# Two of the first expert's three slots, computed while the last gates still run

## The chip, the cores and the metric

The kernel runs on one core of one Trainium2 chip. The metric is the device time of one execution in microseconds (us). Lower is better. A slot, below, is a group of up to 128 tokens of one expert.

## The reference

Attention (4 batches, 8 heads, 576 tokens, 64 columns, the 32 largest scores of each row kept), then a dense layer, then a layer of eight experts of which each token uses one:

```
x = attn_out.transpose(0, 2, 1, 3).reshape(2304, 512)
h = x @ w_in                                   # 512 -> 2048
y = (h * clip(h + 3, 0, 6) / 6) @ w_out        # 2048 -> 512
logits = y @ w_gate                            # 8 experts
expert = argmax(logits); gate_w = softmax(logits)[expert]
out[t] = gate_w[t] * (relu(y[t] @ w1[expert]) @ w2[expert])   # 512 -> 1024 -> 512
```

## The kernel before

Everything is float32. A product is made of three matmuls on numbers split into a high and a low part (`h`, `l`): high by high, high by low, low by high.

**The dense layer** goes over nine blocks of 256 tokens, each in 16 steps of 128 hidden columns. `moe_step` does one step: 12 matmuls of 256 columns into `l1ps` (`l1`, L851), the activation on ACT, DVE and POOL (`gf`, `gh`, `gl`), and six matmuls of 512 columns into `yps` (`l2`, L882). At a block's end ACT copies its two groups of 128 tokens out (`y`, L889).

**The gate** (`gate`) is run for each group of 128 tokens, a part of it in each `gate_step`: four transposes and ACT copies (L902, L903), logits (L910), arg max and softmax on DVE and ACT, two prefix matmuls that give the token's place within its expert (L934, L935), the row `y` to DRAM (`yd`), and the token's number written to a list in DRAM, `td`, at its place (`to_table`, L960).

**The table.** After the last group, `td` is read back into `trow`, the last block's own places are added by PE out of `placed` (`place`, `in128`, which L953 and L955 make), experts are ranked by size (L1169 to L1175), and `tabg` and `tab` (L1184, L1185) list the tokens of each expert's slots. The largest expert is not first: expert 0 is, at rank 0, and the others follow by rank. `ROOM` gives each rank its columns, 384 for the first two, and a slot is at most 128 of them.

**The experts.** `xgather` fetches the rows of an expert's slots from `yd`, one DMA of POOL for each slot (L1200). `xprep` transposes a slot and splits it (`xeh`, `xel`, L1210 to L1213). `m2l1` makes 12 matmuls into `lp` for each of eight `f` steps (L1229), ACT and DVE make `hh` and `hl` of them (L1233, L1234), and `m2l2`, two steps later, makes three matmuls a slot into `ops` (L1246). `m2out` scales a slot on ACT (`osb`, L1253), and POOL scatters it to the output.

**Expert weights** come in eight pieces an expert, each 512 KB: `wload_` loads one into one of three `raw` tiles through SP's queue (L992, L995), and `wpiece` splits it on ACT (`wh`, L1008) and DVE (`wl`, L1009). Pieces 0, 2, 4, 6 are `w1` and 1, 3, 5, 7 are `w2`; piece 2k or 2k+1 serves steps `f` = 2k and 2k+1. Before, `w1` pieces have five tiles of `wh` and of `wl`, and `w2` pieces six. Expert 0's first six pieces are prepared inside the loop of the last steps, the last two after the table's gather.

What sets the order is a scheduler: it takes instructions by a priority that the code sets (`pr`, `tc.cur_priority`), and each engine then executes its own list strictly in that order, waiting where an operand isn't ready.

Of the kernel before, what the change touches and what calls it, by code (L numbers as in the profile page):

```python
# [39 lines left out]
NRAW = 3  # L40
# [17 lines left out]
def attention_two_moe_kernel(  # L58
# [81 lines left out]
    def r_(ap):  # L140
        return ap.bitcast(F32)
# [78 lines left out]
    def body(cs, exact):  # L220
# [9 lines left out]
        m1p = m1.enter_context(tc.tile_pool(name="m1p" + X, bufs=1))  # L230
        ps1 = m1.enter_context(tc.tile_pool(name="ps1" + X, bufs=1, space=PSUM))
        at = ExitStack()
# [651 lines left out]
        def yevac(bk):  # L884
            pr("yevac")
            ys = []
            for tt in range(TB // P):
                y = m1p.tile([P, YW], F32, tag="ysb", bufs=NRAW, name=f"y{bk}_{tt}")
                A.activation(y[:, 0:DM], yps[tt], AF.Copy, scale=1.0 / 6.0)  # L889
                ys.append(y)  # L890
            return ys

        def gate(bk, tt, y):
            pr("gate")
            i = bk * (TB // P) + tt
            last = bk == NBLK - 1
            yt = (wp[0] if last else m1p).tile([P, NCC, P], F32, tag="yt", bufs=1 + last, name=f"yt{i}")
            for hf in range(2):
# [46 lines left out]
            V.tensor_copy(ad, sc[:, 3:4])  # L945
            if last:

                ad2 = m1p.tile([P, 1], I32, tag="ad2", bufs=2, name=f"ad2{i}")
                place, in128 = [wp[0].tile([P, n], F32, tag=f"oh{n}", bufs=2, name=f"oh{n}_{i}") for n in (P, NSL)]
# [48 lines left out]
        def wpiece(e, i):  # L998
            kind, pc = i % 2, i // 2
            if (e, i) not in wraw:  # L1000
                wload_(e, i)
            raw = wraw.pop((e, i))
            late = kind and pc >= NPC // 2
            nb = 3 if kind else 5
            pool = tabp[0] if late else wp[0]
            h = pool.tile([P, 4 * FW], F32R, tag=f"wh{kind}", bufs=nb, name=f"wh{e}_{i}")
            l = pool.tile([P, 4 * FW], F32R, tag=f"wl{kind}", bufs=nb, name=f"wl{e}_{i}")
# [133 lines left out]
        wp[0] = m2.enter_context(tc.tile_pool(name="wp" + X, bufs=1, side="right"))  # L1141
        pre, order = [], [0, 2, 4, 6, 1, 3, 5, 7]
        while gpos[0] < NG + 3 or pend:
            pr0[0] += STEP
            run(moe_step())
            gate_step()
            tc.cur_priority = pr0[0] + STEP
            if gdone[0] == NTT - TB // P and not trows:
                load_table()
            if gpos[0] > NG - 13 and len(pre) < NPC + NPC // 2:  # L1150

                if len(wraw) == 3 or len(pre) + len(wraw) == NPC + NPC // 2:
# [9 lines left out]
        ps2 = m2.enter_context(tc.tile_pool(name="ps2" + X, bufs=1, space=PSUM))  # L1162
# [18 lines left out]
        V.scalar_tensor_tensor(trows[0], tq, part[:, 3:4], cs["row"][0:NSL, :], op0=ALU.subtract, op1=ALU.subtract)  # L1181
        tps = ps2.tile([P, NSL], F32, tag="tp", bufs=2, name="tps")
# [35 lines left out]
        def m2l1(e, f):  # L1218
# [29 lines left out]
        def m2out(e):  # L1248
            gw = xst[e][2]
            for j in range(slots(e)):  # L1250
                m = slot(e, j)
                o = tabp[0].tile([P, DM], F32, tag="osb", bufs=3, name=f"osb{e}_{j}")[0:m]
                A.activation(o, ops_[j][0:m], AF.Copy, scale=gw[0:m, j:j + 1])  # L1253
                si = G.indirect_dma_start(out, bass.IndirectOffsetOnAxis(tab[0:m, e * SLOTS + j:e * SLOTS + j + 1], 0), o, None,
                                          bounds_check=NT - 1, oob_is_err=False)
                tc.declare_no_dep(si.ins, group="out" + X, reason="no token is in two slots")
                tc.add_to_no_dep_group("out" + X, si.ins)

# [146 lines left out]
```

## Time and profile before

| | |
|---|---|
| median of 3 runs | 1214.06 us (1214.02 to 1214.12) |
| the profiled execution | 1211.3 us, its span 1209.4 us |
| mean granted TensorE clock | 0.959 |
| PE busy | 1118.6 us (92%) |
| DVE, ACT, POOL busy | 934.9, 809.0, 459.0 us |

The span is what the trace covers; the rest of an execution, 1.9 us here, lies around it. Start times below are us from the span's start. Engines: PE is TensorE's matmul, PEld its weight loads, DVE the vector engine, ACT the scalar engine, POOL is GpSimd, and SP issues most DMAs.

### The profile page before, as it was taken

What the parts mean: (1) busy time and instruction counts of PE and PEld (TensorE: products, weight loads), DVE (VectorE), ACT (ScalarE), POOL (GpSimd) and SP (SyncE); (2) the same over time, 40 slices, a digit from 0 to 9 for tenths busy, and PEclk for the clock granted to TensorE, in tenths of its full rate; (3) what the DMA queues carried; (4) which work ended last, traced back from release to release, by engine and by line L of the source; (5) the groups of instructions that cost most, each with busy time, mean ns of one, the idle gap of its engine ahead of it and who ended that gap; (6) DMA issues with size and microseconds to landing.
All of it is one profiled execution on the core that took longest, in us unless ns stands there. A gap on an engine that the chain in (4) does not pass through costs nothing.

```text
span 1209.4 us, 24024 instructions
## 1 busy us (share of the span) xinstructions
PE 1118.6 (92%) x7410; PEld 999.2 (83%) x7410; DVE 934.9 (77%) x3821; ACT 809.0 (67%) x2085; POOL 459.0 (38%) x667
## 2 busy tenths in 40 slices
PE   5677688999999999999999999999998799999995
PEld 4566577788899899999988899999887699888894
DVE  4999999999999999998998899998442544444441
ACT  4787878788778788787777788777442444444441
POOL 5886655743322444422343332322353312112110
PEclk9678899999999999999999999999999799999998
DMA  3664566554544555743444554543583755555430
GB/s 77 198 182 135 171 200 209 143 157 135 152 127 127 134 145 154 169 140 114 124 127 139 117 151 134 129 144 103 172 258 109 217 173 175 155 180 185 145 104 17
DMA packets 184122, 179.23 MB, mean 148 GB/s; under 512 B 123629, under 2 KB 148509, under 8 KB 183984
## 3 DMA queue, kind: packets, MB, share of 16 engines
q1 hardware_dynamic: 178960, 167.24, 48.0%
q0 software_dynamic: 3872, 10.08, 2.5%
q8 instruction: 61, 1.00, 0.4%
q14 instruction: 77, 0.63, 0.2%
q10 hardware_dynamic: 1152, 0.28, 0.1%
HBM read 159.53 MB, written 18.61 MB: 147 GB/s over the span
## 4 chain that ended last, share of the span: by engine, by line
PE 74%; DVE 16%; ACT 5%; issue 2%; DMA 1%; POOL 1%; SPq 0%; ACTq 0%; POOLq 0%; DVEq 0%
PE l1ps L851 14%; PE yps L882 14%; PE ops L1246 10%; PE lp L1229 10%; PE ptps L777 9%; PE sps L618 5%; PE ptps L743 4%; DVE cd L648 2%; DVE pbuf L727 2%; DVE z L684 2%; DVE z L719 2%; PE ptps L910 1%; DVE cw L659 1%; DVE m L654 1%; PE misc L462 1%
## 5 line engine op out<-in xcount | busy, mean ns | idle before, releaser
L882 PE MATMUL yps<-wo,gh 128*128 128x512 f32 x576 | 216.5, 417 | 0.5 <-POOL qh L474 0.4
L286 POOL TENSOR_SCALAR gh<-gf 128x256 fp32r<-128x256 f32 x144 | 73.6, 511 | 343.6 <-PE yps L882 215.3
L648 DVE MAX8 cd<-sbuf 128x8 f32<-128x72 f32 x1152 | 187.9, 218 | 3.0 <-ACT sbuf L288 2.7
L851 PE MATMUL l1ps<-xh,wih 128*128 128x256 f32 x576 | 167.4, 291 | 4.5 <-DVE gf L863 2.4
L851 PE MATMUL l1ps<-xh,wil 128*128 128x256 f32 x576 | 163.8, 284 | 0.0
L851 PE MATMUL l1ps<-xl,wih 128*128 128x256 f32 x576 | 163.6, 284 | 0.0
L777 PE MATMUL ptps<-vn,pt 128*128 128x65 f32 (+1 forms) x1152 | 143.6, 278 | 0.0
L777 PEld LDWEIGHTS ptps<-vn,pt 128*128 128x128 f32 x1152 | 140.9, 198 | 0.0
L1009 DVE TENSOR_TENSOR wl<-raw,wh 128x1024 fp32r<-128x1024 f32 x64 | 78.3, 1231 | 79.6 <-ACT wh L1008 71.1
L727 DVE SCALAR_TENSOR_TENSOR pbuf<-sbuf,tall,pbuf 128x576 f32<-128x576 f32 x144 | 138.8, 964 | 0.1
L871 POOL TENSOR_TENSOR gl<-gf,gh 128x256 fp32r<-128x256 f32 x144 | 125.4, 871 | 11.4
L851 PEld LDWEIGHTS l1ps<-xh,wih 128*128 128x128 f32 x576 | 110.0, 191 | 15.2 <-DVE gf L863 7.2
L882 PEld LDWEIGHTS yps<-wo,gh 128*128 128x128 f32 x576 | 107.2, 189 | 16.7 <-POOL qh L474 0.9
L882 PE MATMUL yps<-wo,gl 128*128 128x512 f32 x288 | 116.8, 406 | 0.6 <-POOL gl L871 0.6
L709 ACT ACTIVATE jk<-sbuf,uall 128x576 bf16<-128x576 f32 x144 | 111.7, 775 | 4.2 <-DVE j L723 0.9
L700 ACT ACTIVATE pbuf<-sbuf,nb 128x576 f32<-128x576 f32 x144 | 111.1, 775 | 4.1 <-PE ptps L745 0.9
L851 PEld LDWEIGHTS l1ps<-xl,wih 128*128 128x128 f32 x576 | 110.1, 191 | 4.1
L288 ACT ACTIVATE sbuf<-sps 128x576 f32<-128x576 f32 x144 | 93.0, 646 | 28.8 <-PE sps L618 18.2
L1008 ACT ACTIVATE wh<-raw 128x1024 fp32r<-128x1024 f32 x64 | 67.3, 1059 | 66.1 <-PE lp L1229 31.7
L743 PE MATMUL ptps<-ident,pbuf 128*128 128x128 f32 x576 | 94.9, 288 | 17.6 <-DVE j L723 12.1
L857 ACT ACTIVATE gf<-l1ps,three 128x256 f32<-128x256 f32 x144 | 67.9, 472 | 64.1 <-PE l1ps L851 51.2
L851 PEld LDWEIGHTS l1ps<-xh,wil 128*128 128x128 f32 x576 | 110.4, 192 | 0.1
(237 smaller groups left out, 3006.1 us busy)
## 6 DMA issues: line engine op xcount, KB each, us to landing
wo<-wod SPq DMA_DIRECT2D x144, 512.0 KB, 3.8
raw<-in_moe_w_dram SPq DMA_DIRECT2D x64, 512.0 KB, 3.7
vn<-in_v_dram SPq DMA_DIRECT2D x96, 128.0 KB, 2.7
rawi<-in_moe_w_in_dram SPq DMA_DIRECT2D x16, 512.0 KB, 4.2
rawo<-in_moe_w_out_dram SPq DMA_DIRECT2D x16, 512.0 KB, 4.2
wod<-wc SPq DMA_DIRECT2D x16, 512.0 KB, 5.7
qn<-in_q_dram SPq DMA_DIRECT2D x126, 64.0 KB, 2.9
yd<-y SPq DMA_DIRECT2D x18, 258.0 KB, 5.0
```

The lines of the kernel that those rows point to most:

```text
L288: A.activation(dst, src, AF.Copy)
L648: V.max(cd[:, c, :], s[:, c * CK:(c + 1) * CK])
L700: A.activation(d["p"], d["s"], AF.Exp, bias=d["nb"], scale=SCALE)
L709: A.activation(jk, d["s"][:, 0:S], AF.Sign, bias=ts[t]["u"], scale=-1.0, accum_out=d["sg"])
L727: V.scalar_tensor_tensor(d["p"], d["s"], tall[:, t:t + 1], d["p"], op0=ALU.is_ge, op1=ALU.mult)
L743: PE.transpose(ptps[:, c * P:(c + 1) * P], pb[:, c0 + c * P:c0 + (c + 1) * P], ident)
L777: PE.matmul(d_, a_, b_, start=(i == 0), stop=(i == len(mm) - 1))
L851: PE.matmul(dst, a[:, c, fs], b_[:, c, :], start=(n == 0), stop=(n == 3 * NCC - 1))
L871: G.tensor_tensor(gl, gf, r_(gh), op=ALU.subtract)
L882: PE.matmul(yps[tt], a[:, tsl], b_, start=(f == 0 and m == 0), stop=(f == NF1 - 1 and m == 2))
L1229: PE.matmul(lp, a[:, c, fs], b_[:, c, 0:w], start=(n == 0), stop=(n == 3 * NCC - 1))
L1246: PE.matmul(ops_[j][0:slot(e, j)], a[:, js], b_[:, ns], start=(f == 0 and m == 0), stop=(f == NF2 - 1 and m == 2))
```

## The change

Expert 0's three slots are split. Slots 0 and 1 are filled from the first eight blocks alone, as soon as those are gated: `early_gather` makes a two-column table by PE (from the list of blocks 0 to 6, read from DRAM at the loop's start, and from `placed` for block 7), gathers 256 rows, and `early_prep` transposes them into the idle half of the dense layer's `xbuf`. `early_l1` and `early_l2` then compute them in the dense layer's PSUM (`l1ps`, `yps`), ahead of the table in the code or beside it by priority. What remains of expert 0 (`room(0)` is 128 columns now) is a second pass through all of its weights. The last table no longer reads what blocks 7 and 8 scattered: PE adds both from `placed`. The gate gets two more steps a loop while blocks remain. `wh` and `wl` have four tiles for each kind of piece, and the next expert's pieces are loaded two steps and split four steps into the second pass.

```diff
+    AHEAD = SLOTS - 1
+    def room(r):
+        return ROOM[r] - (r == 0) * AHEAD * P
...
-            if last:
+            if bk >= NBLK - 2:
...
+        def early_gather():
...
+            ops0 = misc([P, AHEAD])
+            for i, a_ in enumerate(trows):
+                PE.matmul(ops0, a_, ident[0:NSL, 0:AHEAD], start=(i == 0), stop=False)
+            for i, (a_, b_) in enumerate(placed):
+                PE.matmul(ops0, a_, b_[:, 0:AHEAD], start=False, stop=(i == len(placed) - 1))
...
+            for j in range(AHEAD):
+                x = m1p.tile([P, YW], F32, tag="ysb", bufs=NRAW, name=f"xa{j}")
+                G.indirect_dma_start(x, None, yd[0:NT - TB, :], bass.IndirectOffsetOnAxis(fg[:, j:j + 1], 0))
+        def early_prep():
...
+                for c in range(NCC):
+                    PE.transpose(tp[:, c, :], x[:, c * P:(c + 1) * P], ident)
...
+        def early_l1(f):
...
+            for c in range(NCC):
+                for a, b_ in ((h, xh), (h, xl), (l, xh)):
+                    PE.matmul(lp, a[:, c, fs], b_[:, c, :], start=(n == 0), stop=(n == 3 * NCC - 1))
...
+            A.activation(hh, lp, AF.Relu)
+            V.scalar_tensor_tensor(hl, lp, 0.0, r_(hh), op0=ALU.max, op1=ALU.subtract)
+        def early_l2(f):
...
+            for j in range(AHEAD):
+                for m, (a, b_) in enumerate(((hh, h), (hl, h), (hh, l))):
+                    PE.matmul(yps[j], a[:, js], b_[:, ns], start=(f == 0 and m == 0), stop=(f == NF2 - 1 and m == 2))
...
-            late = kind and pc >= NPC // 2
-            nb = 3 if kind else 5
-            pool = tabp[0] if late else wp[0]
-            h = pool.tile([P, 4 * FW], F32R, tag=f"wh{kind}", bufs=nb, name=f"wh{e}_{i}")
+            h = wp[0].tile([P, 4 * FW], F32R, tag=f"wh{kind}", bufs=NPC, name=f"wh{e}_{i}")
...
+        load_table()
         while gpos[0] < NG + 3 or pend:
             run(moe_step())
             gate_step()
+            if gpos[0] < NG:
+                gate_step()
+                gate_step()
-            if gdone[0] == NTT - TB // P and not trows:
-                load_table()
+            if gdone[0] == NTT - TB // P and "x" not in ex_:
+                early_gather()
+            if gpos[0] >= NG - 1 and "gw" not in ex_:
+                early_prep()
...
+        for i in order[len(pre) + len(wraw):]:
+            wload_(0, i, ex_["y"])
...
+        pieces = [(e, i) for e in range(1, NE) for i in range(2 * NPC)]
+        for i in range(2):
+            wload_(*pieces[i])
+        xgather(1)
+        for f in range(NF2 + 1):
+            if f < NF2:
+                early_l1(f)
+            if f:
+                early_l2(f - 1)
+            if f == NF2 - 3:
+                xprep(0, 0)
+        for j in range(AHEAD):
+            send(tabp[0].tile([P, DM], F32, tag="osb", bufs=3, name=f"osa{j}"), yps[j], ex_["gw"][:, j:j + 1], ex_["to"][:, j:j + 1])
+        m1s.close()
+        ps2 = m2.enter_context(tc.tile_pool(name="ps2" + X, bufs=1, space=PSUM))
...
-            if s < len(seq) and e + 1 < NE:
-                wpiece(e + 1, f)
+            if 4 <= s < len(pieces) + 4:
+                wpiece(*pieces[s - 4])
+            if 2 <= s < len(pieces):
+                wload_(*pieces[s])
```

Lines move: in the kernel after the change `l1` is L861, `l2` L892, the table L1250 to L1269, `wh` L1082, `wl` L1083, `xprep` L1293 to L1297, `lp` L1312, `hh` and `hl` L1316 and L1317, `ops` L1329, `osb` L1339, and the early pass L1038 (`l1ps`), L1042 (`ha`), L1043 (`la`) and L1053 (`yps`).

Three places show how instructions move. The first is PE's list at the table, before: the second of the last two gates, the table, and the first gathered slot follow each other.

```order
L934 MATMUL ptps_139<-oh17_14400,tri_86 128x8
L935 LDWEIGHTS ones_94
L935 MATMUL ptps_139<-ohsum_123,ones_94 128x8
L1169 LDWEIGHTS ones_94
L1169 MATMUL rk_14461<-ohsum_123,ones_94 24x8
L1178 MATMUL tq_14468<-trow0_14241,ident_79 24x128
...
L1180 MATMUL tq_14468<-oh128_17_14443,oh24_17_14444 24x128
L1183 MATMUL tps_14474<-place_110,trow0_14241 128x24
L1186 MATMUL rk_14461<-place_110,part_107 1x8
L1210 MATMUL tp0_0_14578<-ident_79,xg0_0_14556 128x128 x4
```

The same place on PE after the change (`la`, `ha` are the early pass's `hl`, `hh`):

```order
L946 MATMUL ptps_142<-ohsum_123,ones_94 128x8
L1053 MATMUL yps_141<-wh0_1_14225,ha0_14648 128x512
L1053 MATMUL yps_141<-wh0_1_14225,la0_14649 128x512
L1053 MATMUL yps_141<-wl0_1_14226,ha0_14648 128x512
L1250 LDWEIGHTS ones_94
L1250 MATMUL ptps_142<-ohsum_123,ones_94 24x8
L1053 MATMUL yps_141<-wh0_1_14225,ha1_14664 128x512
L1259 MATMUL ptps_142<-trow0_13806,ident_79 24x128
...
L1261 MATMUL ptps_142<-place17_14500,in128_17_14501 24x128
L1264 MATMUL ptps_142<-place_110,trow0_13806 128x24
L1038 MATMUL l1ps_140<-xh1_151,wh0_2_14128 128x256
```

The early pass's first two `f` steps stand among the gates, its third `l1ps` behind the table's last large matmul (L1264).

DVE's list at the table, before:

```order
L1172 SCALAR_TENSOR_TENSOR place_110,part_107<-place_110,own_106 24x8
L1173 TENSOR_SCALAR place_110,part_107<-place_110,part_107 24x8
L1174 TENSOR_SCALAR part_107<-part_107 24x1
L1181 SCALAR_TENSOR_TENSOR trow0_14241<-tq_14468,part_107,row_102 24x128
L1175 TENSOR_SCALAR place_110<-row_102,part_107 24x24
```

DVE's list at the table, after:

```order
L1253 SCALAR_TENSOR_TENSOR place_110,part_107<-place_110,own_106 24x8
L1083 TENSOR_TENSOR wl0_5_14616<-raw0_5_14509,wh0_5_14615 128x1024
L1254 TENSOR_SCALAR place_110,part_107<-place_110,part_107 24x8
L1262 SCALAR_TENSOR_TENSOR trow0_13806<-ptps_142,part_107,row_102 24x128
L1255 TENSOR_SCALAR part_107<-part_107 24x1
L1083 TENSOR_TENSOR wl0_7_14620<-raw0_7_14512,wh0_7_14619 128x1024
L1256 TENSOR_SCALAR place_110<-row_102,part_107 24x24
```

Two weight pieces now stand between the rows that make `place`.

ACT's list at expert 0's first steps, before:

```order
L1233 ACTIVATE hh0_0_14615<-lp0_0_14602 128x384
L1008 ACTIVATE wh1_0_14621<-raw1_0_14619 128x1024
L1233 ACTIVATE hh0_1_14647<-lp0_1_14634 128x384
L1008 ACTIVATE wh1_1_14653<-raw1_1_14651 128x1024
L1233 ACTIVATE hh0_2_14670<-lp0_2_14657 128x384
L1008 ACTIVATE wh1_2_14685<-raw1_2_14683 128x1024
L1233 ACTIVATE hh0_3_14702<-lp0_3_14689 128x384
```

ACT's list in the second pass, after (DVE's `hl` and `wl` stand in the same order):

```order
L1082 ACTIVATE wh1_0_14942<-raw1_0_14623 128x1024
L1316 ACTIVATE hh0_1_14866<-lp0_1_14853 128x128
...
L1082 ACTIVATE wh1_4_15062<-raw1_4_14946 128x1024
L1316 ACTIVATE hh0_5_14969<-lp0_5_14956 128x128
...
L1082 ACTIVATE wh1_6_15134<-raw1_6_15014 128x1024
L1316 ACTIVATE hh0_7_15029<-lp0_7_15016 128x128
L1082 ACTIVATE wh1_5_15102<-raw1_5_14980 128x1024
L1316 ACTIVATE hh1_0_15055<-lp1_0_15042 128x384
L1082 ACTIVATE wh2_0_15206<-raw2_0_15066 128x1024
L1316 ACTIVATE hh1_1_15090<-lp1_1_15077 128x384
L1339 ACTIVATE osb0_0_15097<-ops0_14833,gw0_14610 128x512
```

The next expert's `wh` stand ahead of the `hh` of steps 1, 5 and 7, and each of them takes the tile of expert 0's piece of the same kind, so `wh1_0` can be written only when `lp0_1`'s matmuls are done with `wh0_0`.

## Rows read from the trace of the kernel before

**Rows 1.** Chain of waits, 926 to 960 us (start us, length us, what)

```profile
926.99 0.02 issue
...
934.38 0.15 PE ptps L934
...
936.93 5.77 DMA td<-tok,ad
...
949.64 5.58 PE lp L1229 x24
```

**Rows 2.** Windows: stretch, length, PE, PEld, DVE, ACT, POOL busy, clock, DMA, GB/s

```profile
930.00:935.00 5.00, 2.86 (x19) 2.53 (x19) 2.11 (x21) 2.09 (x10) 0.40 (x2) 0.68 0.01 3
...
940.00:950.00 10.00, 4.42 (x18) 3.51 (x18) 1.84 (x3) 2.11 (x4) 6.80 (x13) 0.50 0.81 219
950.00:960.00 10.00, 10.00 (x51) 9.37 (x50) 7.33 (x9) 6.81 (x9) 2.66 (x4) 0.89 0.92 305
```

**Rows 3.** Chain of waits, 976 to 1030 us: expert 1 begins

```profile
980.94 2.08 PE lp L1229 x12
...
991.29 2.05 PE ops L1246 x9
...
997.48 0.44 PE tp L1210 x4
```

**Rows 4.** Chain of waits, 840 to 960 us: the dense layer's last blocks

```profile
859.06 1.96 PE ptps L777 x18
...
896.20 0.79 PE ptps L910 x8
...
917.15 1.38 PE yps L882 x6
918.53 1.43 PE l1ps L851 x12
```

**Rows 5.** Groups by line and shape, 905 to 1210 us (count, busy us, mean ns)

```profile
L1009 DVE TENSOR_TENSOR wl<-raw,wh 128x1024 fp32r<-128x1024 f32 x58 | 70.6, 1225 | 74.7 <-ACT wh L1008 68.2 <-PE ops L1246 3.3 <-PE lp L1229 2.9
L1008 ACT ACTIVATE wh<-raw 128x1024 fp32r<-128x1024 f32 x58 | 61.0, 1059 | 64.8 <-PE lp L1229 31.7 <-DMA raw<-in_moe_w_dram 22.3 <-PE ops L1246 7.2
L1229 PEld LDWEIGHTS lp<-xel,wh 128*128 128x128 f32 x256 | 48.5, 189 | 2.1 <-DVE xel L1213 0.2
L1200 POOL DMA_INDIRECT xg<-yd,tabg x22 | 24.3, 1105 | 65.9 <-PE tp L1210 50.7 <-issue 8.9 <-DVE hl L1234 3.6
L1233 ACT ACTIVATE hh<-lp 128x256 fp32r<-128x256 f32 x16 | 6.1, 381 | 20.8 <-PE lp L1229 20.8
L1234 DVE SCALAR_TENSOR_TENSOR hl<-lp,hh 128x256 fp32r<-128x256 f32 x16 | 6.7, 422 | 20.8 <-ACT hh L1233 20.8
L1246 PEld LDWEIGHTS ops<-wl,hh 128*64 128x64 f32 x24 | 3.2, 135 | 2.4
```

**Rows 6.** Timeline of DVE at the table (start, length, line, operation)

```profile
936.33 0.28 DVE L1172 SCALAR_TENSOR_TENSOR place<-place,own 24x8 f32<-24x8 f32 x1
...
937.35 0.34 DVE L1181 SCALAR_TENSOR_TENSOR trow<-tq,part,row 24x128 f32<-24x128 f32 x1 [0.23 <-issue]
937.62 0.25 DVE L1175 TENSOR_SCALAR place<-row,part 24x24 f32<-24x24 f32 x1
```

**Rows 7.** Timeline of SP's queue and of ACT: two weight loads and what they release

```profile
952.51 0.38 SPq L995 DMA_DIRECT2D raw<-in_moe_w_dram  x1
953.75 0.37 SPq L992 DMA_DIRECT2D raw<-in_moe_w_dram  x1
...
956.38 1.06 ACT L1008 ACTIVATE wh<-raw 128x1024 fp32r<-128x1024 f32 x1 [0.62 <-DMA raw<-in_moe_w_dram]
958.96 1.06 ACT L1008 ACTIVATE wh<-raw 128x1024 fp32r<-128x1024 f32 x1 [0.20 <-DMA raw<-in_moe_w_dram]
```

**Rows 8.** Page, DMA issues (count, size, median us to landing)

```profile
raw<-in_moe_w_dram SPq DMA_DIRECT2D x64, 512.0 KB, 3.7
```

**Rows 9.** Chain of waits at the end: the last expert's slots leave

```profile
1194.09 0.63 ACT osb L1253
...
1194.77 0.70 ACT osb L1253
...
1195.51 0.19 PE ctlp L1296 x2
```

More of the change, by code (lines that the diff above doesn't have):

```diff
@@ L230, in body @@
         m1p = m1.enter_context(tc.tile_pool(name="m1p" + X, bufs=1))
-        ps1 = m1.enter_context(tc.tile_pool(name="ps1" + X, bufs=1, space=PSUM))
+        m1s = ExitStack()
+        ps1 = m1s.enter_context(tc.tile_pool(name="ps1" + X, bufs=1, space=PSUM))
+        m1w = ExitStack()
+        w1p = m1w.enter_context(tc.tile_pool(name="m1w" + X, bufs=1))
         at = ExitStack()
@@ L890, in yevac @@
                 ys.append(y)
+            ex_["y"] = y
             return ys
@@ L896, in gate @@
             last = bk == NBLK - 1
-            yt = (wp[0] if last else m1p).tile([P, NCC, P], F32, tag="yt", bufs=1 + last, name=f"yt{i}")
+            yt = (wp[0] if last and tt else m1p).tile([P, NCC, P], F32, tag="yt", bufs=1, name=f"yt{i}")
             for hf in range(2):
@@ L945, in gate @@
             V.tensor_copy(ad, sc[:, 3:4])
-            if last:
+            if bk >= NBLK - 2:
                 ad2 = m1p.tile([P, 1], I32, tag="ad2", bufs=2, name=f"ad2{i}")
-                place, in128 = [wp[0].tile([P, n], F32, tag=f"oh{n}", bufs=2, name=f"oh{n}_{i}") for n in (P, NSL)]
+                place = m1p.tile([P, TB], F32, tag="gf", bufs=2, name=f"place{i}")[:, 0:P] if last else \
+                    wp[0].tile([P, P], F32, name=f"place{i}")
+                in128 = wp[0].tile([P, NSL], F32, name=f"in128_{i}")
                 V.tensor_scalar(ad2, ad, P - 1, None, op0=ALU.bitwise_and)
@@ new lines, in early_prep @@
+        def early_prep():
+            xh, xl = xbuf[NBLK % 2]
+            gw = m1p.tile([P, AHEAD], F32, name="gwa")
+            ex_["gw"] = gw
+            for j, x in enumerate(ex_["x"]):
+                tp = sps[:, j, :].rearrange("p (c q) -> p c q", c=NCC)
+                for c in range(NCC):
+                    PE.transpose(tp[:, c, :], x[:, c * P:(c + 1) * P], ident)
+                sl = slice(j * P, (j + 1) * P)
+                A.activation(xh[:, :, sl], tp, AF.Copy)
+                V.tensor_tensor(xl[:, :, sl], tp, r_(xh[:, :, sl]), op=ALU.subtract)
+                G.tensor_copy(gw[:, j:j + 1], x[:, DM:DM + 1])
@@ new lines, in early_l1 @@
+        def early_l1(f):
+            xh, xl = xbuf[NBLK % 2]
+            h, l = [i.rearrange("p (c f) -> p c f", c=NCC) for i in wst[0, 0, f // FPP]]
+            fs = slice((f % FPP) * P, (f % FPP + 1) * P)
+            lp = l1ps[:, f % 2, :]
+            n = 0
+            for c in range(NCC):
+                for a, b_ in ((h, xh), (h, xl), (l, xh)):
+                    PE.matmul(lp, a[:, c, fs], b_[:, c, :], start=(n == 0), stop=(n == 3 * NCC - 1))
+                    n += 1
+            hh = m1p.tile([P, TB], F32R, tag="gh", bufs=2, name=f"ha{f}")
+            hl = m1p.tile([P, TB], F32R, tag="gl", bufs=2, name=f"la{f}")
+            A.activation(hh, lp, AF.Relu)
+            V.scalar_tensor_tensor(hl, lp, 0.0, r_(hh), op0=ALU.max, op1=ALU.subtract)
+            ex_[f] = (hh, hl)
@@ L1166, in body @@
         rank = part[:, 4:8]
-        rk = ps2.tile([P, 256], F32, name="rk")
-        cnt = rk[0:NSL, 0:NE]
+        cnt = ptps[0:NSL, 0:NE]
         PE.matmul(cnt, ones[:, 0:NSL], ohsum, start=True, stop=True)
@@ L1175, in body @@
         V.tensor_scalar(place_, cs["row"][0:NSL, 0:NSL], rank[:, 2:3], None, op0=ALU.is_equal)
-        tq = ps2.tile([NSL, P], F32, tag="tp", bufs=2, name="tq")
+        tq = ptps[0:NSL, P:2 * P]
         for i, a_ in enumerate(trows):
@@ L1185, in body @@
         V.tensor_copy(tab, tps)
-        PE.matmul(rk[0:1, 16:16 + NE], part[:, 1:2], place_.rearrange("p (e s) -> p e s", s=SLOTS)[:, :, 0], start=True, stop=True)
-        V.tensor_copy(cs["list"], rk[0:1, 16:16 + NE])
+        by_rank = ptps[0:1, 3 * P:3 * P + NE]
+        PE.matmul(by_rank, part[:, 1:2], place_.rearrange("p (e s) -> p e s", s=SLOTS)[:, :, 0], start=True, stop=True)
+        V.tensor_copy(cs["list"], by_rank)
         for r in range(1, NE):
@@ L1235, in m2l1 @@
             hst[e, f] = (hh, hl)
-        ops_ = [ps2.tile([P, DM], F32, name=f"ops{j}") for j in range(SLOTS)]
+        ops_ = []
         def m2l2(e, f):
@@ L1252, in m2out, with send @@
                 o = tabp[0].tile([P, DM], F32, tag="osb", bufs=3, name=f"osb{e}_{j}")[0:m]
[L1253 to L1257, printed above, removed]
+                send(o, ops_[j][0:m], gw[0:m, j:j + 1], tab[0:m, column(e, j):column(e, j) + 1])
+        def send(o, ps, gw, to):
+            A.activation(o, ps, AF.Copy, scale=gw)
+            si = G.indirect_dma_start(out, bass.IndirectOffsetOnAxis(to, 0), o, None, bounds_check=NT - 1, oob_is_err=False)
+            tc.declare_no_dep(si.ins, group="out" + X, reason="no token is in two slots")
+            tc.add_to_no_dep_group("out" + X, si.ins)
         xgather(0)
@@ L1262, in body @@
         for i in range(2 * NPC):
-            if i not in pre and (0, i) not in wraw:
-                wload_(0, i, xst[0][3][0])
-        for i in range(2 * NPC):
             if i not in pre:
                 wpiece(0, i)
-        for j in range(SLOTS):
-            xprep(0, j)
+        pieces = [(e, i) for e in range(1, NE) for i in range(2 * NPC)]
[13 more added lines that the diff above has]
+        ps2 = m2.enter_context(tc.tile_pool(name="ps2" + X, bufs=1, space=PSUM))
+        ops_.extend(ps2.tile([P, DM], F32, name=f"ops{j}") for j in range(SLOTS))
         seq = [(e, f) for e in range(NE) for f in range(NF2)]
@@ L1274, in body @@
                 if e + 1 < NE:
-                    if f == (e == 0):
+                    if f == 1 and e:
                         xgather(e + 1)
```

45 lines of the change are left out of this document (34 added, 11 removed).

## The prediction

> **What bounds the kernel now.** The page comes first: PE is busy 92% of the span, so the question is where the other 8% lies, and whether the change is there. The chain of waits shows it for the stretch of the change. After the last block's `l2` (926.99) the chain leaves PE: gates until the second prefix matmul at 934.38, the scatter to `td` at 936.93 (5.77 us), gather, transposes, and the first expert's `lp` at 949.64 [rows 1]. So PE does no matmul of the dense layer or of an expert for 22.65 us. The windows show the second loss: the granted clock is 0.68 and 0.89 in the neighbouring stretches and 0.50 in between [rows 2], 0.50 being 1.2 GHz and 1.00 2.4 GHz. The first two `lp` groups take 5.58 us [rows 1], where two of the same form take 4.16 later [rows 3]. From 980.94 on PE steps from `lp` to `ops` without any wait [rows 3].
>
> I therefore make the sum for one stretch of PE: from the end of block 8's `l2` (926.99) to expert 1's first `ops` (991.29), **64.3 us** before [rows 1, 3], plus what is added ahead of it. Behind it, PE does the same as before. The sum stands against the profiled execution, 1211.3 us, which lies 2.8 us (0.23%) under the median of the runs; the difference found is put on the median, 1214.06. A measurement of this kernel can tell about 0.2%, 2.4 us, from no change.
>
> **A: added ahead of block 8's end.** Eight transposes of `early_prep` at 0.11 (four take 0.44 [rows 3]) are 0.9. The two-column table is four fp32 matmuls, eight in the trace's count, at 0.10 (eight take 0.79 [rows 4]): 0.8. They stand in PE's full list, so they push it. POOL's two gathers, 1.1 each [rows 5], stand ahead of the dense layer's `gh` and `gl` there; POOL has slack in a step and I cost them at nothing, or at 2.2 if it has none. For waits of the table's short DVE steps I take 0.7. A is **2.4**, between 1.7 and 4.6. The two further `gate_step` calls a loop move block 7's gates earlier and add no work. `td`'s read at the loop's start, and the removed read after the scatter, are off PE's path.
>
> **B: early pass with the last gates and the table.** Each of eight `f` steps is one `l1ps` group of the dense layer's form (1.43) and one `yps` group (1.38) [rows 4]: 22.5. The gates' eight transposes are 0.9, their 16 logits matmuls at 0.10 1.6, the table's seven fp32 matmuls and two small ones about 1.6, one `xprep` 0.44 [rows 3]. Work: 27.0. The gates' chain still has waits that the first two early steps don't fill; I take 1.4 (zero to 4).
>
> A new wait comes from DVE's list. The second prefix matmul starts 7.4 after the block's end [rows 1]; as early steps and faster logits offset each other, I take 7.3. From that matmul to the end of L1172 is 2.2 (934.38 to 936.61) [rows 1, 6], so L1253 ends at 9.5. In DVE's list `wl0_5` comes next, 1.23 [rows 5], then L1254 0.2, `trow` 0.3, L1255 0.2, `wl0_7` 1.23, L1256 0.25 (short ones as their like [rows 6]): 12.9. Only then can PE run L1264, and everything behind it, from the early pass's third `l1ps` on, waits as well. What PE has ahead of L1264 is two `l1ps` (2.9), one `yps` and a matmul of the next (1.6), the gates (2.5) and most of the table (1.5), with the waits 9.9. The wait is **3.0**; if the two pieces didn't stand there, it would be 0.5. B is **31.4**.
>
> **C: the boundary.** The second pass's `lp` and `ops` take the PSUM that `yps` leaves, so `lp0_0` waits for both `osa` copies on ACT. The kernel's end has the same two copies: 1194.02 to 1195.51 [rows 9], **1.5**.
>
> **D: the second pass, to expert 1's first `ops`.** No row has an fp32r `lp` group of 128 columns. The bounds are 1.43 (256 columns [rows 4]) and 0.79, by columns: 384 columns take 2.08, 256 take 1.43, so 128 less is 0.65. I take 1.32, as 18 matmuls of 65 columns take 1.96 [rows 4] and four transposes of 128 columns 0.44 [rows 3]: 0.11 each whatever the columns, which is a weight load's time. A load of 128 columns of weights shows 189 ns and one of 64 shows 135 [rows 5]; 54 ns for 64 columns is 108 for 128. The Trainium skill ("TensorE: Matmul & The Clock Gate", LDWEIGHTS) gives columns / 1.2 GHz, 107 ns, which those rows bear out; its section on the back-to-back gap says a stream of 128-column matmuls runs at 81 ns each, which no row here shows: by that the pass would have 2.8 us less of work, and with the chain of loads below the time would be 1211.8.
>
> Work: eight times 1.32 and 0.69 (half of a `yps` group) are 16.1, three `xprep` 1.3, three `lp` of expert 1 6.2: 23.6. But the weights of expert 1 don't fit beside it. Before, `lp` and `ops` of 384 columns and three slots took 4.1 a step (2.08 and 2.05 [rows 3]), beside one piece; now a step is 2.0, and a piece a step is still to be split. Reckon from `lp0_0` at 0. `wh1_0` overwrites `wh0_0`, so it starts behind `lp0_1`, at 2.7; `hh0_1` and `hl0_1` stand behind it and `wl1_0`, and `lp0_3` starts at 5.35, 0.7 late. `wh1_2` follows `lp0_3`'s end (6.7), `wl1_2` ends at 9.05. That frees the `raw` tile for `raw1_4`, and a chain begins: load 3.9 (952.51 to 956.38 [rows 7]; the median is 3.7 [rows 8]), `wh` 1.06, `wl` 1.23 [rows 5], hand-overs 0.1, so 6.3 a round. `wl1_4` ends at 15.3, `wl1_6` at 21.6, and `raw2_0` lands at 25.5. ACT has `hh0_5`, `hh0_7` and finally `hh1_1` and `osb0` behind these `wh`, DVE `hl0_5` and `hl0_7` behind the `wl`. So `lp0_7` is late by 0.95, `lp1_1` by 1.4, and expert 1's first `ops` waits for `osb0`: `raw2_0` 25.5, `wh2_0` 26.6, `hh1_1` 27.1, `osb0` 27.8. D is **27.8**, 4.2 of it waits. Later, a step is 4.1 and the chain of 6.3 for two steps is covered.
>
> **Sum.** 2.4 + 31.4 + 1.5 + 27.8 = 63.1, against 64.3: **1.2 less**, 1212.9. The change fills the gap of 22.65 us, but reads expert 0's weights a second time on PE: splitting 384 columns into 256 and 128 costs (1.43 + 1.32 − 2.08) × 8 = 5.4, and the rest goes into waits.
>
> **Rivals.**
> *The waits are mostly filled* (0.17). B and D hold 8.6 us of them. Against it: each is a fixed place in an in-order list. For it: the gates' 1.4 and the table's 3.0 rest on when DVE and the loads of `raw0_5` and `raw0_7` really come. Half of them gone: 1208.6; all: 1204.3.
> *128-column matmuls are priced by columns* (0.11): 0.79 a group is 4.2 less work, 1208.7 were it all kept. But the chain of loads starts only 1.6 earlier and then sets the end: 1211.3.
> *Slower: loads in the chain take 5.2* (0.18), as the one issued 1.24 behind another did (953.75 to 958.96, at 305 GB/s [rows 2, 7]). In the second pass loads come in pairs too, with `xg` gathers and output scatters beside them. Three rounds, 1.33 each: +4.0, 1216.9. It decides from landings of about 5.0 on: three times 1.2 is what separates 1212.9 from 1216.5.
> *The clock falls in B's wait* (0.10): before, it fell in a stretch of gates where PE was busy 2.86 of 5 us [rows 2]. The first groups after it would cost 5.58 for 4.16 [rows 1, 3]: +1.4, 1214.3. Against it: early steps surround the wait.
>
> The sum itself has 0.44, and 1210.4 to 1215.6 as its own range (A's, C's and the gates' bounds). **Faster by over 0.2%** (under 1211.6): nearly all of the first rival, two thirds of the second, a quarter of the sum's case, 0.34. **Slower by over 0.2%** (over 1216.5): most of the slower rival, and a little of the clock's, 0.20. Within: 0.46. The range, 1207.5 to 1218, leaves out the best of the first rival and landings over 5.6.
>
> **What would show it.** Early `l1ps` and `yps` between about 929 and 958; a wait of some 3 us on DVE's `place` ahead of the third early `l1ps`; 1.5 on `osa` before `lp0_0`; twelve matmuls of 128 columns in about 1.3; `lp0_3`, `lp0_7`, `lp1_1` and expert 1's first `ops` waiting for `hl` and `osb`, with `raw1_4`, `raw1_6`, `raw2_0` each issued at the end of the `wl` before. The granted clock stays at 1.00 from 927 on. The prediction is wrong if the table's wait is filled, if the loads of the chain are off 3.9 by more than half a us, or if a wait stands where I have none, above all in A, where POOL's gathers could hold `gh`.

## The result and the profile after

The change made the kernel slower: 1222.81 us median (6 runs, 1219.38 to 1226.81) against 1214.04 (6 runs, 1211.89 to 1215.47), a ratio of **1.0073**, 95% interval 1.0051 to 1.0096. A later set of four runs of the same kernel (e12) gave 1.0046 (1.0028 to 1.0064). The forecast was 1212.9, in a range of 1207.5 to 1218. The profiled execution took 1224.55 us.

The page of the profile of the changed kernel, first line and busy times, and below it the same line of its second profile (e12). The span grows by 13.1 us, and PE is busy 9.7 us longer. That is not work alone, since at a low clock the same matmuls take longer: in the second profile PE is busy only 2.8 us longer than before.

```profile
span 1222.5 us, 24268 instructions
...
PE 1128.3 (92%) x7519; PEld 1007.9 (82%) x7519; DVE 933.4 (76%) x3847; ACT 806.4 (66%) x2093; POOL 463.3 (38%) x667
...
PE 1121.4 (92%) x7519; PEld 1001.6 (82%) x7519; DVE 936.2 (77%) x3847; ACT 806.3 (66%) x2093; POOL 463.3 (38%) x667
```

PE's waits from the dense layer's last steps to expert 1, as the view of waits lists them (us in total, how many, the longest). Before, it lists none from 860 to 927.

```profile
PE ptps L1264 <- DVE place L1256: 2.3, 1, 2.3
PE l1ps L861 <- DVE gf L873: 1.5, 2, 1.0
PE ops L1329 <- ACT osb L1339: 1.5, 1, 1.5
PE yps L892 <- POOL y L938: 1.5, 1, 1.5
PE lp L1312 <- ACT osa L1339: 1.4, 1, 1.4
PE yps L892 <- POOL gh L296: 0.9, 1, 0.9
PE yps L892 <- POOL gl L881: 0.8, 2, 0.5
PE lp L1312 <- DVE hl L1317: 0.4, 1, 0.4
PE yps L1053 <- ACT ha L1042: 0.3, 1, 0.3
```

The table's wait (L1264), the boundary (`osa`) and expert 1's `osb` are where the prediction had them. The lines with `gf`, `gh`, `gl` and `y` are not: they lie ahead of block 8's end. Windows of the same profile (columns as in [rows 2]) show where PE stood still, and what the clock did:

```profile
905.00:910.00 5.00, 3.21 (x20) 2.43 (x18) 0.42 (x1) 0.48 (x2) 3.16 (x5) 1.00 0.92 252
910.00:915.00 5.00, 3.61 (x20) 2.83 (x21) 0.42 (x1) 0.74 (x2) 1.79 (x5) 1.00 0.59 210
...
945.00:950.00 5.00, 2.69 (x18) 1.87 (x18) 4.80 (x22) 0.67 (x1) 2.95 (x2) 1.00 0.18 59
950.00:955.00 5.00, 5.00 (x27) 4.42 (x27) 0.72 (x5) 0.38 (x1) 3.85 (x4) 0.66 0.55 112
...
970.00:975.00 5.00, 3.65 (x28) 3.52 (x27) 0.29 (x1) 2.01 (x4) 2.03 (x2) 0.89 0.27 105
975.00:980.00 5.00, 5.00 (x22) 4.71 (x22) 1.72 (x3) 1.03 (x3) 0.00 (x0) 0.50 0.34 108
980.00:985.00 5.00, 5.00 (x26) 4.60 (x26) 2.98 (x4) 2.83 (x4) 0.86 (x1) 0.59 0.09 18
985.00:990.00 5.00, 5.00 (x40) 4.64 (x40) 2.61 (x6) 3.42 (x6) 1.90 (x3) 1.00 0.89 285
```

Two things stand out: 3.2 of 10 us without PE from 905 to 915, and the clock at 0.66 behind the table's wait and at 0.50 in the second pass, with PE full. In the second profile (e12) the clock falls already where PE stands still in the dense layer:

```profile
905.00:910.00 5.00, 1.69 (x4) 1.15 (x5) 0.42 (x1) 0.47 (x1) 3.17 (x5) 0.91 0.77 261
910.00:915.00 5.00, 5.00 (x26) 4.47 (x25) 0.42 (x1) 0.47 (x1) 2.87 (x7) 0.75 0.29 105
```

What POOL does there, in the timeline of the first profile:

```profile
900.80 0.73 POOL L881 TENSOR_TENSOR gl<-gf,gh 128x256 fp32r<-128x256 f32 x1
906.34 1.02 POOL L1014 DMA_INDIRECT xa<-yd,fg  x1 [4.81 <-DVE gf L873]
907.67 0.95 POOL L1014 DMA_INDIRECT xa<-yd,fg  x1 [0.30 <-issue]
908.65 0.41 POOL L296 TENSOR_SCALAR gh<-gf 128x256 fp32r<-128x256 f32 x1
...
913.07 0.18 POOL L1028 COPY gwa<-xa 128x1 f32<-128x1 f32 x1 [3.19 <-DMA xa<-yd,fg]
913.23 0.40 POOL L296 TENSOR_SCALAR gh<-gf 128x256 fp32r<-128x256 f32 x1
```

POOL stands still twice: 4.81 us ahead of the first early gather, and 3.19 us ahead of the copy of the gathered rows' gate column, each time with the dense layer's `gh` next in its list. The 4.81 is put down to `gf`, which the gather does not read; the second profile of the same kernel (run e12) names a DMA, the rows of block 7 on their way to `yd`:

```profile
905.20 1.02 POOL L1014 DMA_INDIRECT xa<-yd,fg  x1 [6.54 <-DMA yd<-y]
...
910.00 0.18 POOL L1028 COPY gwa<-xa 128x1 f32<-128x1 f32 x1 [1.25 <-DMA xa<-yd,fg]
```

The first profile has that write too, and its time from issue to landing: it landed at about 905.5, and the gather, 0.9 later, was the next thing that POOL did.

```profile
896.78 0.37 SPq L950 DMA_DIRECT2D yd<-y  x1
...
DMA to landing us min/median/max: 8.7/8.7/8.7
```

To compare kernels I cut the span at four points of PE's timeline: **S**, the start of the 19th `l1ps` group from the dense layer's end; **E**, the end of its last `yps`; **L**, the first `lp` of expert 0's (second) pass; **O**, expert 1's first `ops`. The prediction's terms are S to E for A, E to L for B and C, L to O for D. One profile each (us):

```
                      S-E    E-L    L-O   O-end   span
before               62.4   22.5   41.7   218.3  1209.4
by the prediction    64.8   32.9   27.8   218.3
changed              70.4   34.8   31.2   219.8  1222.5
e12 changed again    71.6   35.8   28.1   219.9  1219.0
e1  rows late        71.0   35.9   28.2   220.3  1221.2
e11 copy late        71.0   35.9   29.2   220.2  1219.8
e5  both             66.0   36.2   28.4   220.0  1213.8
e2  wl on POOL       71.7   37.3   28.1   219.7  1220.1
e6  wl after table   70.4   31.1   28.5   219.9  1215.0
e3  four raw         70.9   34.8   24.7   219.7  1215.0
e4  own PSUM         70.5   34.6   28.2   220.0  1220.8
e7  one gate_step    69.6   34.8   28.2   219.2  1217.2
e9  fill             71.8   33.6   29.5   219.7  1217.1
e8  all five         66.8   29.7   24.6   219.6  1208.6
e10 all, one step    66.9   29.6   24.5   219.4  1209.0
```

Where an edit doesn't touch a stretch, the stretch stays within 1 to 2 us, as long as the clock does; I read effects of a few us from here, and from ratios only where intervals part. The spans of single profiles can't be compared so closely: ahead of S, where the kernels with the change do the same, it takes from 862.6 us (e9, mean clock 0.97) to 868.6 (e10, 0.96).

### The profile page after: what moved, and what is told of

The parts are those of the page before. It is cut to its first block, busy times and chain, and to the rows that moved or that the text cites. A ratio compares the mean times of both kernels' runs of the same rounds, so it can differ in the third digit from the quotient of the medians.

```text
span 1222.5 us, 24268 instructions
## 1 busy us (share of the span) xinstructions
PE 1128.3 (92%) x7519; PEld 1007.9 (82%) x7519; DVE 933.4 (76%) x3847; ACT 806.4 (66%) x2093; POOL 463.3 (38%) x667
## 3 DMA queue, kind: packets, MB, share of 16 engines
q8 instruction: 62, 1.02, 0.3%
## 5 line engine op out<-in xcount | busy, mean ns | idle before, releaser
L892 PE MATMUL yps<-wo,gh 128*128 128x512 f32 x576 | 217.5, 417 | 2.5 <-POOL y L938 1.5
L861 PE MATMUL l1ps<-xh,wih 128*128 128x256 f32 x576 | 166.5, 289 | 7.0 <-DVE gf L873 5.4
L861 PE MATMUL l1ps<-xh,wil 128*128 128x256 f32 x576 | 163.3, 284 | 0.0
L861 PE MATMUL l1ps<-xl,wih 128*128 128x256 f32 x576 | 163.0, 283 | 0.0
L1083 DVE TENSOR_TENSOR wl<-raw,wh 128x1024 fp32r<-128x1024 f32 x64 | 78.3, 1223 | 101.2 <-ACT wh L1082 101.2
L737 DVE SCALAR_TENSOR_TENSOR pbuf<-sbuf,tall,pbuf 128x576 f32<-128x576 f32 x144 | 136.2, 946 | 0.1
L1082 ACT ACTIVATE wh<-raw 128x1024 fp32r<-128x1024 f32 x64 | 67.7, 1058 | 86.8 <-PE lp L1312 60.5
L861 PEld LDWEIGHTS l1ps<-xh,wih 128*128 128x128 f32 x576 | 109.2, 190 | 17.3 <-DVE gf L873 9.5
L892 PEld LDWEIGHTS yps<-wo,gh 128*128 128x128 f32 x576 | 107.3, 190 | 18.8 <-POOL y L938 1.7
L892 PE MATMUL yps<-wo,gl 128*128 128x512 f32 x288 | 117.1, 407 | 1.4 <-POOL gl L881 1.4
L861 PEld LDWEIGHTS l1ps<-xl,wih 128*128 128x128 f32 x576 | 109.1, 189 | 4.3
L861 PEld LDWEIGHTS l1ps<-xh,wil 128*128 128x128 f32 x576 | 109.2, 190 | 0.1
```

The lines of the kernel that those rows point to most:

```text
L737: V.scalar_tensor_tensor(d["p"], d["s"], tall[:, t:t + 1], d["p"], op0=ALU.is_ge, op1=ALU.mult)
L861: PE.matmul(dst, a[:, c, fs], b_[:, c, :], start=(n == 0), stop=(n == 3 * NCC - 1))
L892: PE.matmul(yps[tt], a[:, tsl], b_, start=(f == 0 and m == 0), stop=(f == NF1 - 1 and m == 2))
```

## The experiments

Theory 1: the excess over the forecast lies ahead of block 8's end, where POOL waits for DMAs with the dense layer's work behind it. Theory 2: it lies in the second pass, in its chain of loads and its clock. In the code shown, `...` stands for lines left out.

**e1: gathers later.** The gathers' indices are made to depend on a later `gf`, two to three steps on, and DVE copies the gate column.

```diff
+            V.tensor_scalar(late[:, 0:AHEAD], gst[gpos[0] - 2][:, 0:AHEAD], 0.0, None, op0=ALU.mult)
+            V.tensor_tensor(fg, ex_["fg"], late[:, 0:AHEAD], op=ALU.add)
...
-                G.tensor_copy(gw[:, j:j + 1], x[:, DM:DM + 1])
+                V.tensor_copy(gw[:, j:j + 1], x[:, DM:DM + 1])
```

> Changed kernel, with the two early gathers issued two to three steps of the dense layer later, when the rows of block 7 have landed, and the gate column copied by DVE instead of POOL. Theory 1 (POOL stands still at the early gathers until block 7's rows are in DRAM, and the dense layer's gh behind them holds PE): PE's waits on POOL between 905 and 915 us go, block 8's last l2 ends about 4 us nearer to its first steps (66 us from the first step of the loop instead of 70), and the time falls by 3 to 4.5 us, to a ratio of 1.004 to before. Theory 2 (the excess over the forecast lies in the second pass, its chain of loads and its low clock): the time stays within 1 us of the changed kernel, 1.007.

Measured: 1.0073 (1.0054 to 1.0091), S to E 71.0. No gain, against theory 1 as I had put it. But PE's waits on POOL were gone, and its waits on DVE's `gf` had grown to 4.0 us, the longest 2.9. That line, and DVE's timeline, which says why:

```profile
PE l1ps L861 <- DVE gf L873: 4.0, 2, 2.9
...
916.18 0.15 DVE L1036 COPY gwa<-xa 128x1 f32<-128x1 f32 x1 [2.55 <-DMA xa<-yd,fgl]
919.47 0.15 DVE L1036 COPY gwa<-xa 128x1 f32<-128x1 f32 x1 [3.14 <-DMA xa<-yd,fgl]
919.55 0.41 DVE L873 SCALAR_TENSOR_TENSOR gf<-gf,l1ps 128x256 f32<-128x256 f32 x1
```

The two copies stood early in DVE's list, ahead of a `gf`, and DVE waited there for the landing. My edit had moved the wait to another engine.

**e5: both.** As e1, with the copy made to depend on `early_prep`'s last result:

```diff
-                V.tensor_copy(gw[:, j:j + 1], x[:, DM:DM + 1])
+                V.tensor_scalar(z, r_(xl[:, 0, j * P:j * P + 1]), 0.0, None, op0=ALU.mult)
+                V.tensor_tensor(gw[:, j:j + 1], x[:, DM:DM + 1], z, op=ALU.add)
```

> The kernel of e1_rows_late, with the gate column of the early rows copied only after early_prep has split them, so that no engine stands still for the gathers' landing. Theory 1 (what holds PE is an in-order engine that waits for a DMA: in e1 the copy on DVE took over the wait from POOL): from the loop's first step to block 8's last l2 it is 66 to 67 us, against 71.0 in e1 and 70.4 in the changed kernel, and the time falls by 3.5 to 4.5 us, ratio 1.004. Theory 2 (PE loses the time elsewhere in the loop): 70 us and 1.007 again.

Measured: S to E **66.0**, within the 66 to 67 of theory 1. PE has no wait on POOL left, one of 0.9 on `gf`, and is full from 905 to 915:

```profile
PE l1ps L861 <- DVE gf L873: 0.9, 1, 0.9
...
905.00:910.00 5.00, 5.00 (x35) 4.56 (x34) 0.77 (x4) 0.74 (x2) 2.07 (x3) 1.00 0.82 274
910.00:915.00 5.00, 5.00 (x33) 4.30 (x32) 0.84 (x2) 0.68 (x2) 4.07 (x9) 1.00 0.82 271
```

The ratio, 1.0052 (1.0029 to 1.0074), can't be told from the changed kernel's own two, so the gain is shown in the profile and not in the time of this run alone.

**e11: only the copy late.** The copy of e5, with the gathers where the change has them.

> Changed kernel, with the early gathers where they are, and only the gate column's copy made late, as in e5. It parts the hold on POOL in two: the wait ahead of the gathers (block 7's rows on their way to DRAM) stays, the wait behind them (the gathered rows landing) goes. If the first is most of it, the loop's last nine steps keep 14 to 15 us from the ninth to the fifth from the end (11.3 in e5, 15.5 in the changed kernel) and the ratio is 1.006; if the second is, they take 12 to 13 and the ratio is 1.005.

Measured: 1.0055 (1.0038 to 1.0072), S to E 71.0, ninth to fifth step from the end 16.0 (15.5 and 16.9 in the changed kernel's two profiles). The first wait, for block 7's rows, is enough by itself; with it in place the second costs nothing that shows.

**e3: four `raw` tiles.** The free space beside the experts' tiles takes a fourth.

```diff
-            wraw[e, i] = raw = wp[0].tile([P, 4 * FW], F32, tag="raw", bufs=3, name=f"raw{e}_{i}")
+            pool, nb = (tabp[0], 4) if e else (wp[0], 3)
+            wraw[e, i] = raw = pool.tile([P, 4 * FW], F32, tag="raw", bufs=nb, name=f"raw{e}_{i}")
```

> Changed kernel, with four raw tiles for the weights of experts 1 to 7 in place of three. Theory 2: the second pass is set by the chain load, wh, wl through one tile, so it ends 4 to 5 us earlier (26 to 27 us from lp0_0 to expert 1's first ops, from 31.2), ratio 1.0035. Theory 1: the chain is only what is left behind the low clock, and with wh still waiting for the old tile's last reader the gain is under 1.5 us, ratio 1.006 to 1.007.

Measured: 1.0049 (1.0030 to 1.0068), L to O **24.7**. That is 6.5 less than the first profile of the changed kernel, but 3.4 less than its second one: the chain costs 3.4, and the rest was the clock (e12).

**e12: the changed kernel again.**

> The changed kernel itself, a second profile. The second pass took 31.2 us from lp0_0 to expert 1's first ops in its first profile, of which some 3 us lay in a stretch at 0.50 of the clock; with the clock at 1.00 it should take 28 to 28.5, as in e1, e2 and e4. If it takes 31 again at 1.00, the clock was not the reason.

Measured: L to O 28.1 with the clock at 1.00 from 960 to 1000. So the first profile's 31.2 held 3 us of low clock, and the chain is as forecast. Two of its loads in the chain of waits of e12:

```profile
980.20 3.48 DMA raw<-in_moe_w_dram
...
992.22 4.73 DMA raw<-in_moe_w_dram
```

**e2: `wl` of pieces 5 and 7 on POOL.**

```diff
-            V.tensor_tensor(l, raw, r_(h), op=ALU.subtract)
+            (G if (e, i) in ((0, 5), (0, 7)) else V).tensor_tensor(l, raw, r_(h), op=ALU.subtract)
```

> Changed kernel, with wl of expert 0's pieces 5 and 7 made by POOL instead of DVE, so that nothing long stands between the rows that make place. If those two pieces are what the table's matmul waits for, the wait of 2.3 us at L1264 falls to under 0.5, and if the clock's fall behind it (950 to 953) comes from that wait, another 1.2 is gained: 3 to 3.5 us, ratio 1.0045. If the clock falls there anyway: 2 us. If the wait only moves, to POOL's gather of slot 2 behind the two wl, nothing.

Measured: 1.0114 (1.0091 to 1.0137), and PE's wait at L1264 4.0 instead of 2.3. A miss, and none of the three outcomes that I had named. PE's wait, then DVE and POOL in e2's timeline:

```profile
PE ptps L1264 <- DVE place L1256: 4.0, 1, 4.0
...
945.83 4.55 DVE L1256 TENSOR_SCALAR place<-row,part 24x24 f32<-24x24 f32 x1
...
945.63 4.70 POOL L1083 TENSOR_TENSOR wl<-raw,wh 128x1024 fp32r<-128x1024 f32 x2
```

DVE's 24x24 comparison, 0.25 before [rows 6], took as long as POOL's two operations. The Trainium skill ("SBUF — State Buffer", SBUF: two separate sides) says that GpSimd and some of DVE's operations share a pair of ports as an exclusive lock: whichever starts first has it for its whole instruction, and the other is blocked. These rows agree that DVE stood still while POOL worked, 4.55 beside 4.70; but they show it blocked through two of POOL's instructions, not one.

**e6: the same two pieces after the table.** They stay on DVE, and one column of each is first written from `tps`, which ties them to L1264.

```diff
+            if (e, i) in ((0, 5), (0, 7)):
+                V.tensor_copy(l[:, 0:1], tps[:, 0:1])
             V.tensor_tensor(l, raw, r_(h), op=ALU.subtract)
```

> Changed kernel, with wl of pieces 5 and 7 on DVE again, but held until the table's matmul L1264 is done, so that neither DVE nor its neighbour POOL does long work in the table. If those two pieces made the wait: L1264's wait under 0.7 us instead of 2.3, the clock stays at 1.00 behind it (1.2 us more), ratio 1.0045. If e2's longer wait (4.0) came from something other than POOL's work beside DVE, the wait stays over 2 us here too and the ratio at 1.007.

Measured: no wait at L1264, E to L **31.1**, 3.7 to 4.7 less than in the changed kernel's two profiles, clock 1.00 from 930 on. The ratio is 1.0042 (1.0017 to 1.0066), not apart from theirs. The windows at the table's wait, now without one:

```profile
945.00:950.00 5.00, 5.00 (x36) 4.16 (x34) 3.38 (x17) 0.38 (x1) 3.01 (x3) 1.00 0.35 17
950.00:955.00 5.00, 5.00 (x33) 4.46 (x32) 1.96 (x3) 0.77 (x2) 4.15 (x5) 1.00 0.52 111
```

**e4: `l1ps` and `yps` in a PSUM pool of their own**, closed after the others, so that `lp` doesn't wait for `osa`.

```diff
+        ps1r = m1r.enter_context(tc.tile_pool(name="ps1r" + X, bufs=1, space=PSUM, side="right"))
...
-        l1ps = ps1.tile([P, 2, TB], F32, name="l1ps")
+        l1ps = ps1r.tile([P, 2, TB], F32, name="l1ps")
```

> Changed kernel, with l1ps and yps in a PSUM pool of their own, so that the second pass's lp need not wait for the two osa copies. The wait of 1.4 us before lp0_0 goes in either case. If that gap is what makes the clock fall to 0.50 from 974 to 984 us, the low stretch goes too, and the second pass takes 28 instead of 31.2: in all 4 us, ratio 1.004. If the clock falls without the gap, 1 to 1.5 us, ratio 1.006.

Measured: 1.0061 (1.0040 to 1.0082); the wait of 1.4 is gone, but E to L is 34.6, while the clock stood at 0.51 and 0.81 for ten us behind the table's wait. What the gap at the boundary does to the clock it doesn't settle: e1, e2 and e12 have the gap and a clock of 1.00 behind it.

**e9: PE kept busy in two waits** by matmuls that nobody reads.

```diff
+        busy = misc([P, P])
+        for i in range(9):
+            PE.matmul(busy, placed[-1][0], placed[-1][0], start=True, stop=True)
...
+                last_ = ex_[f - 1]
...
+        for i in range(12):
+            PE.matmul(l1ps[:, 0, :], last_[1][:, 0:P], last_[0], start=True, stop=True)
```

> Changed kernel, with matmuls that nobody reads put into two of PE's waits: nine of 128x128 fp32 ahead of L1264 (about 2 us, the wait there is 2.3) and twelve of 256 columns between the early pass and lp0_0 (1.4 us, the wait for osa is 1.4). They add work and no order. If the clock falls because PE stands still there, it stays at 1.00 behind both places, the times of one run to the next lie closer together, and the median falls by 1.5 to 3 us, ratio 1.005 to 1.006. If the clock falls for another reason, the time is that of the changed kernel or up to 0.5 us more.

Measured: 1.0058 (1.0037 to 1.0078), not apart from the changed kernel's. In the profile the clock stays at 1.00 from 915 to 990, and E to L, with more work and the table no sooner, falls to 33.6. The clock fell where waits were not filled: behind one of 2.6 us in the second pass, at 990, and behind the dense layer's, 3.0 us for POOL:

```profile
900.00:905.00 5.00, 3.42 (x24) 2.92 (x22) 0.42 (x1) 0.47 (x1) 1.10 (x2) 1.00 0.79 200
905.00:910.00 5.00, 3.60 (x9) 2.62 (x10) 0.42 (x1) 0.47 (x1) 3.31 (x8) 0.55 0.51 163
...
945.00:950.00 5.00, 4.90 (x36) 4.32 (x36) 3.06 (x15) 0.38 (x1) 2.80 (x3) 1.00 0.22 18
950.00:955.00 5.00, 5.00 (x35) 4.48 (x34) 0.54 (x2) 0.67 (x2) 2.49 (x6) 1.00 0.73 194
```

**e7: one further `gate_step` a loop, not two.**

> Changed kernel, with one further gate_step a loop instead of two. If the denser gates cost PE its waits on DVE's gf between the loop's first step and the ninth from the end (36.9 us there, 33.8 before), this stretch shortens by 1 to 1.5 us and the ratio is 1.006. If they cost nothing, the gathers only come later, the hold on POOL of about 4 us stays, and the time is within 0.7 us of the changed kernel.

Measured: 1.0047 (1.0027 to 1.0067). S to the ninth step from the end is 36.0 against 36.9 and 36.7: less than expected, and not clear.

**e8: e5, e6, e3 and e4 in one**, and **e10: the same with e7.**

> Rows gathered late, copy late, wl after the table, four raw tiles, PSUM of its own: all in one. Theory 1 and 2 give the same sum if their parts add: 4 (gathers and copy) + 3 (table) + 3.4 (chain of loads) + 1.4 (boundary) = 11.8 us less than the changed kernel, a ratio of 0.9975 to before. If the early pass itself costs more than the sum gave it (the split into 256 and 128 columns, 5.4, and more), it stays at 1.000 or above.

> The kernel of e8_all_five (0.9967) with one further gate_step a loop instead of two, as in e7. If e7's gain was the denser gates' cost, another 1 us is gained in the loop, ratio 0.996; if it was only that the hold at the gathers came at a better place, which e8 has removed, nothing is.

Measured: **0.9967** (0.9952 to 0.9982) and **0.9955** (0.9938 to 0.9972). Both beat the kernel before, by 0.3% and 0.45%; from each other they can't be told, and S to E is no shorter in e10, so what the denser gates cost doesn't show. The parts add: S to E, E to L and L to O come within 1 us of the values of e5, e6 (less the 1.4 of e4) and e3. The waits that PE has left in e8:

```profile
PE l1ps L863 <- DVE gf L875: 1.5, 2, 1.3
PE lp L1329 <- DVE hl L1334: 0.4, 1, 0.4
PE yps L1065 <- ACT ha L1054: 0.3, 1, 0.3
```

## Why the prediction was wrong

The likeliest case (1212.9) failed by 9.9 us, beyond the range. Between the two profiles it was 14.4 (1224.55 against 1211.3 less 1.2), of which 2.8 and 1.7 are how far the two profiled executions lie from their medians. By stretches, the first profile is over the forecast by 5.6 in A, 1.9 in B and C, 3.4 in D, 1.5 behind O and 1.8 ahead of S; the second (e12) by 6.8, 2.9, 0.3 and 1.6, and 1.0 under it ahead of S. The largest part, and the one that stays, is A.

**A failed.** "POOL has slack in a step and I cost them at nothing, or at 2.2 if it has none": I counted what POOL does for the gathers (1.1 each; 1.02 and 0.95 measured), not what it waits for. The gather needs block 7's rows in DRAM. `yd`'s last write of that block was issued at 896.78, the gather started at 906.34, and `gh` stood behind it. S to E grew by 8.0 and 9.2 instead of 2.4; e5 takes 4.4 to 5.6 of it away, and e8 and e10, which hold the same edits, have 66.8 and 66.9, so the mechanism is shown. A part of it is the clock, which falls behind this wait too: in e12 it loses 1.7 of the 10 us from 905 to 915 (0.91 and 0.75), in the first profile nothing, and in e5, e8 and e10 it stays at 1.00 there. Of the 3.6 that are left in e5, 1.7 are the transposes and the table, 0.9 a wait on `gf` behind a `wl`; 1 us I can't place. The prediction ended with this wait as what could prove it wrong, but the wait itself had no term in the sum, no chance, and no place in the range.

**B and C held, but for the clock.** Forecast 32.9, measured 34.8 and 35.8. The table's wait is 2.3 (3.0 forecast), on the row named, 12.6 behind block 8's end (12.9), and the boundary 1.4 (1.5):

```profile
949.26 0.40 PE L1264 MATMUL ptps<-place,trow 24*128 24x24 f32 x2 [2.31 <-DVE place L1256]
```

The clock fell behind the table's wait, the rival that I gave 0.10 and 1.4 us; it came in each profile that had this wait unfilled, and e6 and e9 show it gone with the wait. The reason that I held against it, "early steps surround the wait", was wrong.

**D held.** 27.8 forecast, 28.1 to 28.5 at full clock in e1, e2, e4 to e7 and e12 (29.5 and 29.2 in e9 and e11, where the clock was below 1.00 near 990). Twelve matmuls of 128 columns take 1.33 (0.11 each), from the start of one group to that of the next in e12, so the rival that prices them by columns fell:

```profile
972.38 0.27 PE L1312 MATMUL lp<-xeh,wh 128*128 128x128 f32 x1
...
973.71 0.28 PE L1312 MATMUL lp<-xeh,wh 128*128 128x128 f32 x1
```

The 81 ns that the Trainium skill ("TensorE: Matmul & The Clock Gate", Back-to-back issue gap) gives does not agree with these rows either. The waits are the ones named. e3 removes the chain: 24.7, beside 23.6 of work. The slower rival, three landings of 5.2, came in part: of the two loads that the chain of waits shows in each profile with three `raw` tiles, one took 3.4 to 3.7 (4.6 in e11) and the other 4.7 to 5.25. By the prediction's own sign, loads off 3.9 by more than half a us, the second one failed; that D came out so close is in part luck, as the first was shorter. In the first profile a low clock took 3 us here, which I had not allowed for in the second pass.

**"PE does the same as before" failed by 1 to 2 us.** O to the end is 219.2 to 220.3 in all kernels with the change, 218.3 in the one profile before. I don't know why, and no experiment was made for it.

The sum's other side was right: the gap is filled, and the work costs about what it was given. With those waits taken out (e8), E to O is 54.3, where the forecast had 52.0 without its waits at the table, the boundary and the chain (27.0 and 1.4 in B, 23.6 in D), and 64.2 before. With the three stalls (the early gathers, the table and the chain of loads) and the boundary taken out, the change gives 0.3 to 0.45%.

## What to carry to other kernels

When work is moved ahead on an engine that executes in order, price each instruction by what it waits for, not by its own length: a DMA issued or a copy made at the wrong place of a list stops everything behind it, and moving only that instruction to another engine moves the stop. Tie early work to a late operand, so that it comes in the list where its data is really there, and then ask of every new wait of PE what the clock does behind it.

## What was not expected of the hardware

A DVE operation of 0.25 us took 4.55 while POOL worked through two operations of 128x1024 beside it (e2).

A DRAM write of 258 KB took 8.7 us to land (before the first early gather), where the page of the same profile has a median of 5.4 for its like.

The clock fell behind some waits of PE and not behind others of like length: behind 2.3 us at the table in each profile that had it unfilled, behind 1.4 us at the boundary in one of several, and behind the dense layer's wait for POOL in the second profile of the changed kernel (3.2 us) but not in the first (1.5 and 0.9). The time of a run follows it: of e5's twelve runs, the five with a mean granted clock of 0.967 or more took 1214.6 to 1216.9 us, the seven at 0.965 or less 1218.8 to 1225.3. In e8, with hardly a wait left, twelve runs lay between 1207.5 and 1211.4.
